# Sinkhorn-sorted attention and a token mixer on one core: batch 1's V turned on TensorE, half of the first q loaded in fp32, q of batches 1 and 2 turned in full tiles, a new order

## The chip, the cores and the metric

The kernel runs on one core of a Trainium2 chip. Its time is device microseconds of one execution, the median of several runs. The engines are TensorE (PE in the profile, its weight loads PEld), VectorE (DVE), ScalarE (ACT), GpSimd (POOL) and SyncE (SP), which here only issues DMAs. Batches are counted from 0 in all that follows; the change's own short title counts them from 1 where it says "batches 2 and 3".

## The reference

```python
B, H, S, D = 4, 8, 768, 64          # n_blocks = 8, block = 96, all inputs fp32
P = sort_net                        # (B, H, 8, 8)
for _ in range(5):                  # Sinkhorn
    P = exp(P - P.max(-1)); P /= P.sum(-1) + 1e-9; P /= P.sum(-2) + 1e-9
k_sorted = einsum('bhij,bhjcd->bhicd', P, k_blocks)      # blocks of 96 tokens
v_sorted = einsum('bhij,bhjcd->bhicd', P, v_blocks)
scores = q_blocks @ k_sorted_blocks.T / sqrt(D)          # within each block
attn = softmax(scores)
x = (attn @ v_sorted_blocks)  ->  (B, S, H * D)          # (4, 768, 512)
wq, wk = x @ w_q, x @ w_k                                # (4, 768, 64)
mixed = (wq @ wk.T / sqrt(64)) @ x                       # over all tokens of a batch
out = relu(mixed) @ w_out                                # (4, 768, 512)
```

## The kernel before

All of the core's work is written as units, one letter each, and one string, `ORDER` (lines 18 to 48), lists the units of all engines; the program issues them in that sequence. Each engine works through its own units strictly in this order, and a unit waits only for the data and for the PSUM banks that it needs. A unit is written as letter, batch, number, and then, for a unit on TensorE, the first PSUM bank that it writes (capitals: `K21:3` is the K unit of batch 2, head pair 1, into banks 3 and 4) or the engine (`k21:D:3` takes it out with VectorE; A is ScalarE, G GpSimd, S the SP queue).

The units, in the order of one batch's path:

- `l` issues a load. Each tensor of a batch (q, k or v, 1.57 MB in fp32) is one DMA on POOL's queue that casts to bf16 on its way (`u_l`, line 206). Three buffers stand for each of q, k and v, so batch 3 uses batch 0's. `lp` and `lo` load the mixer's weights.
- `a`, `c`, `p`, `B`, `u`, `n`: Sinkhorn for all 32 matrices at once, VectorE and ScalarE taking turns, then `n` spreads the result to M (line 232), the matrices with which K and V are sorted. `Z` are filler matmuls without use for the result.
- `Q`, `q`: q of a pair of heads turned on TensorE, twelve transposes of half tiles (128x64) a pair, then taken out to QT. For batch 3, GpSimd copies each pair to a contiguous place (`C`, line 360), and an SP transposing DMA turns it (`D` with number 4 and up, line 364).
- `K`, `k`: k sorted and turned in one go, twelve matmuls a pair against M, and taken out to KT.
- V goes one of two ways. In batch 0, `Y` does for V what `K` does for k (into the other batch's KT buffer), and `F` turns it back with eight transposes, `f` takes it to VT. In batches 1 to 3, `V` sorts it without turning (three units of eight matmuls), `v` takes it to Vs, and six SP DMAs `R` (line 301) rearrange it from Vs to VT; number n of `R` is one of six rows of 16 partitions, and every P of the batch needs all six.
- `S`, `e`: scores of five head-block pairs and their Exp on ScalarE. `P`, `r`, `x`: attention times V with a column of ones, its reciprocal and the product on VectorE.
- `T`, `t`: x turned on TensorE for batches 0 to 2; for batch 3 four SP transposing DMAs (`D` with numbers 0 to 3).
- `J`, `j`, `d`, `W`, `w`, `G`, `g`, `H`, `h`, `O`, `o`: the mixer; `O` and `o` give the output in six row groups of a batch, `s` stores them (`u_s`, line 434). `PAIRED` names the stores that go as one DMA of two row groups.

Queues to keep in mind: POOL issues all loads and in the same sequence makes M for later batches, the copies C and small copies d. SP issues all R, D and s, in order. In the old order the last lines of the loads are `lq2 .. lv3 .. lq3 .. lk3`: k of batch 3 is loaded last. On SP, the order near the last batch is `D37 R35 D36 R33 D35 R34 R32 D34`.

Of the kernel before, what the change touches and what calls it, by code (L numbers as in the profile page):

```python
# [22 lines left out]
n21:G e02:A:0 S01:6 f02:D:2 S06:3 e01:A:6 S00:0 n20:G F00:5 e06:A:3 V12:6 f00:D:5 e00:A:0 S04:2 lk2 v12:D:6
P01:4 e04:A:2 S05:0 lo r01:D:4 e05:A:0 R15:S P00:6 x01:D:4 lv2 S03:2 R14:S V10:0 e03:A:2 r00:D:6 lq2 P03:4
x00:D:6 v10:A:0 P04:2 lv3 r03:D:4 r04:D:2 K12:6 x03:D:4 P02:0 k12:A:6 x04:D:2 V11:4 r02:D:0 T03:7 x02:D:0
v11:A:4 T00:6 K11:2 t00:D:6 T01:0 R12:S lq3 k11:A:2 t03:D:7 T02:4 R11:S t01:A:0 Q13:6 Q11:7 lk3 R10:S Q12:5
t02:A:4 q11:D:7 Q10:0 R13:S K13:1 q10:A:0 J00:7 n31:G q12:A:5 S12:3 j00:D:7 J01:0 e12:A:3 k13:D:1 d00:G W00:7
j01:A:0 q13:D:6 K10:3 w00:A:7 d01:D n30:G k10:A:3 S14:0 S13:6 W01:2 e13:A:6 w01:D:2 K21:3 G00:2 e14:A:0
k21:D:3 S10:6 e10:A:6 K22:0 K20:3 k22:D:0 G01:2 k20:A:3 S11:6 g00:D:2 K23:0 e11:A:6 H01:2 k23:D:0 h01:A:2
P12:4 S16:6 S15:0 r12:D:4 e16:A:6 x12:D:4 P10:2 e15:A:0 O03:7 r10:D:2 x10:D:2 o03:A:7 V22:0 H00:4 v22:A:0  # L30
V20:6 h00:D:4 P11:2 v20:A:6 R25:S V21:0 r11:D:2 H02:4 x11:D:2 v21:A:0 R20:S P13:6 R21:S h02:A:4 r13:D:6 P14:0
x13:D:6 T11:2 R23:S Q20:3 R24:S Q21:4 r14:D:0 q20:A:3 Q23:7 R22:S q21:D:4 Q22:6 x14:D:0 S21:3 q22:A:6 O05:5
q23:D:7 e21:A:3 t11:D:2 T13:7 S22:0 t13:D:7 S20:3 e22:A:0 T12:6 O04:7 t12:D:6 e20:A:3 T10:6 o04:A:7 S24:0
t10:D:6 S26:2 O00:4 e26:A:2 o05:D:5 e24:A:0 V30:6 o00:A:4 S23:2 v30:D:6 S25:0 J10:5 e25:A:0 J11:4 R31:S
j10:A:5 P21:0 e23:A:2 R30:S d10:G W10:7 V32:5 r21:D:0 j11:A:4 x21:D:0 P23:2 w10:A:7 O02:4 v32:A:5 C31:G
r23:D:2 x23:D:2 P22:0 d11:A C33:G o02:A:4 P20:6 W11:5 r22:D:0 V31:2 x22:D:0 C30:G w11:A:5 D37:S O01:4 v31:A:2
C32:G r20:D:6 P24:0 x20:D:6 T22:5 o01:A:4 T21:2 R35:S t22:A:5 G10:3 r24:D:0 t21:D:2 D36:S K30:6 x24:D:0 K32:4
k30:A:6 G11:3 k32:D:4 K33:0 R33:S g10:A:3 K31:6 k33:A:0 D35:S H10:2 k31:D:6 T20:4 h10:A:2 T23:5 S35:0 R34:S
t23:D:5 S34:6 e35:A:0 H12:2 t20:D:4 R32:S O10:5 D34:S h12:A:2 J20:0 o10:D:5 e34:A:6 J21:1 j20:D:0 s00:S S36:4
s02:S S32:2 j21:D:1 S33:6 e36:A:4 s01:S W20:0 e32:A:2 d21:G P33:4 w20:D:0 d20:G O11:0 e33:A:6 r33:D:4 x33:D:4  # L40
W21:1 P34:2 w21:A:1 P32:6 r34:D:2 o11:A:0 x34:D:2 S31:4 G20:1 s10:S e31:A:4 r32:D:6 D33:S x32:D:6 S30:2 G21:1
H11:4 g20:A:1 D32:S P31:6 e30:A:2 O14:0 r31:D:6 x31:D:6 h11:A:4 P30:1 O15:3 o14:A:0 r30:D:1 D31:S x30:D:1
# [9 lines left out]
def kernel(  # L52
# [93 lines left out]
    def copy(e, o, i):  # L146
        if e == "A":
            nc.scalar.copy(o, i)  # L148
        else:
            nc.vector.tensor_copy(o, i)  # L150
# [34 lines left out]
    def u_i(b, n, e, bank):  # L185
# [9 lines left out]
        elif n == 3:  # L195
# [7 lines left out]
                nc.gpsimd.memset(t[:, :, :, D:DV], 1.0)  # L203
            nc.gpsimd.memset(Rall[:, :, NG - 1, :, (NU - AG * (NG - 1)) // 2:AG // 2], 1.0)

    def u_l(b, n, e, bank):
        if n == "p":
            for s, w in enumerate((moe_w_q, moe_w_k)):
                nc.gpsimd.dma_start(out=wqk[:, :, s, :], in_=w.rearrange("(t p) d -> p t d", p=P))  # L209
        elif n == "o":  # L210
            nc.gpsimd.dma_start(out=wo, in_=moe_w_out.rearrange("(t p) d -> p t d", p=P))  # L211
        else:
            t, src = {"q": (Qn, q), "k": (Kn, k), "v": (Vn, v)}[n[0]]
            h0, h1 = {"": (0, H), "a": (0, H // 2), "b": (H // 2, H)}[n[2:]]
            b = int(n[1])
            nc.gpsimd.dma_start(out=t[b % NIN][:, h0:h1].rearrange("p h r d -> p h (r d)"),  # L216
                                in_=src[b, h0:h1].rearrange("h (p r) d -> p h (r d)", p=P))
# [139 lines left out]
    def pairs(b, n):  # L357
        return Qn[(b + 1) % NIN].rearrange("p h r d -> p (h r d)")[:, n * 2 * R6 * D:(n + 1) * 2 * R6 * D]

    def u_C(b, n, e, bank):  # L360
        nc.gpsimd.tensor_copy(pairs(b, n).rearrange("p (r h d) -> p r h d", r=R6, h=2),
                              Qn[b % NIN][:, 2 * n:2 * n + 2].rearrange("p h r d -> p r h d"))

    def u_D(b, n, e, bank):
# [292 lines left out]
```

## Time and profile before

| | |
|---|---|
| time, median of 3 runs | 98.78 us (98.74 to 98.85) |
| the profiled execution | 99.26 us, of which the span is 97.4 us |
| granted TensorE clock, mean | 0.995 |
| busy: TensorE, VectorE, ScalarE, GpSimd | 84.3, 66.7, 70.7, 30.9 us |
| transfers: casting loads on POOL's queue | 14064 packets, 10.09 MB, 68.7% of 16 engines' span |
| transfers: SP's queue | 12064 packets, 10.31 MB, 39.2% |

The views of the profile that follow are: the page (busy time of each engine, the span in 40 slices, the chain that ended last); the chain in order of time (start, length, what); windows (busy time of each engine in a stretch, with instruction counts in brackets); groups of instructions (line, engine, operation, result and sources with shapes, count, then busy us and mean ns of one, then idle time before them and what ended it); the timeline (start us, length us, engine and line, count, in square brackets the idle time before it and what ended it); and the view of a tile (its instructions with their least, median and longest duration in ns, first and last start, and for DMAs the time from issue to landing). Buffer numbers are left out there: Qn, Kn and Vn are all buffers of q, k and v. All copies out of PSUM have the helper's lines, 148 for ScalarE and 150 for VectorE, and all matmuls line 144.

### The profile page before, as it was taken

The numbers are of one execution on the slowest core, as the hardware profiler recorded it, in microseconds if no ns is written. First come the engines' busy times: TensorE is split into PE (matmuls) and PEld (weight loads), VectorE is DVE, ScalarE is ACT, GpSimd is POOL, SyncE is SP. The second block draws the span as 40 slices with busy tenths as digits, with TensorE's granted clock in tenths as the row PEclk, the third lists the DMA queues.
The fourth block names the chain that finished last, engine by engine and source line by source line (L and its number), as shares of the span: only waits on it lengthen the run. The fifth ranks groups of instructions, "written<-read, shape, count | busy, mean of one in ns | idle before, by whom it ended". The sixth has DMA issues, their size and how long they took to land.

```text
span 97.4 us, 3326 instructions
## 1 busy us (share of the span) xinstructions
PE 84.3 (87%) x1396; PEld 58.2 (60%) x1406; DVE 66.7 (68%) x133; ACT 70.7 (73%) x102; POOL 30.9 (32%) x50
## 2 busy tenths in 40 slices
PE   4953978979898988988999999999899999999950
PEld 1323567868787576747965688984676545643410
DVE  2677985859993567879877569996596897625300
ACT  5411199999877899979789999899968644558450
POOL 5994009999406750000000086000300480000000
PEclk9999999999999999999999999999999999999997
DMA  0799999999999999999999999788999893691983
GB/s 3 76 197 203 203 205 208 199 204 204 207 221 205 235 248 205 204 204 206 211 249 250 222 201 235 131 170 101 295 423 312 90 247 142 252 391 73 398 315 120
DMA packets 26144, 20.62 MB, mean 212 GB/s; under 512 B 8336, under 2 KB 23440, under 8 KB 26128
## 3 DMA queue, kind: packets, MB, share of 16 engines
q0 software_dynamic: 14064, 10.09, 68.7%
q1 hardware_dynamic: 12064, 10.31, 39.2%
q8 instruction: 11, 0.18, 0.7%
q14 instruction: 5, 0.04, 0.1%
HBM read 20.19 MB, written 6.29 MB: 272 GB/s over the span
## 4 chain that ended last, share of the span: by engine, by line
PE 44%; DMA 32%; POOL 9%; ACT 5%; issue 3%; SPq 2%; DVE 1%; ACTq 0%; POOLq 0%; DVEq 0%
PE ps L144 44%; DMA Vn<-in_v_dram 20%; DMA Qn<-in_q_dram 8%; POOL M L240 5%; DMA VT<-Vs 4%; ACT KT L148 2%; POOL wqk L209 2%; SPq L366 1%; DVE mixT L421 1%; ACT ot L148 1%; ACT Vs L148 1%; ACT QT L148 1%; POOL Kn L216 1%; SPq L302 1%; POOL wo L211 1%
## 5 line engine op out<-in xcount | busy, mean ns | idle before, releaser
L316 ACT ACTIVATE E<-ps 96x960 bf16<-96x960 f32 (+1 forms) x28 | 24.1, 897 | 1.7 <-PE ps L144 1.4
L144 PE MATMUL ps<-wo,mixT 128*128 128x512 bf16 x87 | 22.3, 379 | 0.8 <-issue 0.3
L345 DVE TENSOR_TENSOR X<-ps,Rall 96x896 bf16<-96x896 f32 (+1 forms) x20 | 20.0, 1005 | 0.6
L144 PEld LDWEIGHTS <-mixT 128*128 128x128 bf16 x96 | 8.3, 97 | 9.2 <-issue 0.8
L148 ACT COPY ot<-ps 128x512 f32<-128x512 f32 x17 | 9.9, 586 | 4.8 <-PE ps L144 4.3
L144 PE MATMUL ps<-VT,E 96*128 96x65 bf16 x256 | 10.9, 193 | 1.0 <-DMA VT<-Vs 0.4
L144 PEld LDWEIGHTS <-E 96*128 96x128 bf16 x256 | 9.5, 97 | 3.1 <-issue 2.1
L382 POOL COPY qD<-qkT 64x384 bf16<-64x384 bf16 x4 | 2.0, 502 | 29.0 <-ACT qkT L148 20.1
L148 ACT CAST KT<-ps 128x768 bf16<-128x768 f32 x12 | 9.3, 804 | 1.4 <-PE ps L144 1.0
L240 POOL TENSOR_TENSOR M<-PTR,m_p 128x512 bf16<-128x512 bf16 x6 | 7.8, 1310 | 7.3 <-ACT KT L148 6.1
L144 PEld LDWEIGHTS <-KT 64*128 64x128 bf16 (+1 forms) x288 | 8.3, 97 | 2.9 <-issue 1.2
L144 PE MATMUL ps<-QT,KT 64*128 64x96 bf16 x256 | 9.2, 204 | 0.0
L150 DVE CAST KT<-ps 128x768 bf16<-128x768 f32 x8 | 7.6, 955 | 2.1 <-PE ps L144 2.0
L144 PE MATMUL ps<-M,Kn 128*64 128x128 bf16 x192 | 7.5, 220 | 1.4 <-DMA Kn<-in_k_dram 0.4
L419 ACT ACTIVATE mixT<-ps 128x1024 bf16<-128x1024 f32 x8 | 8.2, 1025 | 0.6 <-PE ps L144 0.6
L150 DVE COPY ot<-ps 128x512 f32<-128x512 f32 x7 | 4.8, 690 | 4.0 <-PE ps L144 3.7
L148 ACT CAST Vs<-ps 128x1024 bf16<-128x1024 f32 x7 | 6.9, 1017 | 0.9 <-PE ps L144 0.8
L144 PEld LDWEIGHTS <-Kn 128*64 128x64 bf16 x192 | 6.3, 109 | 2.0 <-DMA Kn<-in_k_dram 0.8
L144 PE MATMUL ps<-fil 128*128 128x512 bf16 x21 | 6.3, 464 | 1.4 <-DVE fil L192 1.2
L144 PE MATMUL ps<-idb,Qn 128*64 128x128 bf16 x144 | 4.8, 220 | 2.8 <-DMA Qn<-in_q_dram 2.8
L421 DVE TENSOR_SCALAR mixT<-ps 128x1024 bf16<-128x1024 f32 x4 | 4.8, 1222 | 2.5 <-PE ps L144 2.3
L144 PEld LDWEIGHTS <-Qn 128*64 128x64 bf16 x144 | 4.1, 110 | 3.9 <-DMA Qn<-in_q_dram 3.4
(80 smaller groups left out, 130.8 us busy)
## 6 DMA issues: line engine op xcount, KB each, us to landing
out_dram<-ot SPq DMA_DIRECT2D x18, 256.0 KB, 2.2
Qn<-in_q_dram POOLq DMA_DIRECT2D x4, 768.0 KB, 22.5
Vn<-in_v_dram POOLq DMA_DIRECT2D x4, 768.0 KB, 18.0
Kn<-in_k_dram POOLq DMA_DIRECT2D x4, 768.0 KB, 16.9
VT<-Vs SPq DMA_DIRECT2D x18, 132.0 KB, 6.3
out_dram<-ot SPq DMA_DIRECT2D x3, 512.0 KB, 4.3
wo<-in_moe_w_out_dram POOLq DMA_DIRECT2D x1, 512.0 KB, 16.7
wqk<-in_moe_w_q_dram POOLq DMA_DIRECT2D x1, 64.0 KB, 14.3
```

The lines of the kernel that those rows point to most:

```text
L144: nc.tensor.matmul(o, w, x, is_transpose=t, start=start, stop=stop, skip_group_check=True)
L148: nc.scalar.copy(o, i)
L150: nc.vector.tensor_copy(o, i)
L209: nc.gpsimd.dma_start(out=wqk[:, :, s, :], in_=w.rearrange("(t p) d -> p t d", p=P))
L211: nc.gpsimd.dma_start(out=wo, in_=moe_w_out.rearrange("(t p) d -> p t d", p=P))
L216: nc.gpsimd.dma_start(out=t[b % NIN][:, h0:h1].rearrange("p h r d -> p h (r d)"), in_=src[b, h0:h1].rearrange("h (p r) d -> p h (r d)", p=P))
L240: ENG[e].tensor_tensor(out=M[b % 2][:, h0:h0 + hn], in0=src.unsqueeze(2).to_broadcast([P, hn, SP, NB]), in1=m_p.unsqueeze(1).unsqueeze(3). ...
L316: nc.scalar.activation(E[b % 2][:, n, 0:2 * w * BLK].rearrange("p (t a c) -> p a t c", a=2, c=BLK), PS[0:BLK, bank:bank + 2, 0:w * BLK].re ...
L345: nc.vector.tensor_mul(xo.rearrange("p (a t d) -> p a t d", a=2, d=D), avps(bank, w)[:, :, :, 0:D], Rall[:, b, n, :, 0:w].unsqueeze(3).to_ ...
L382: nc.gpsimd.tensor_copy(o, i)
L419: nc.scalar.activation(o, i, ACT.Relu)
L421: nc.vector.tensor_relu(o, i)
```

## The change

1. V of batch 1 goes the way of batch 0: `Y`, `y`, `F`, `f` in place of `V`, `v` and the six `R`.
2. q of batch 0 is loaded in halves. Heads 0 to 3 come as fp32 on ScalarE's DMA queue (`lf`) into a mixer buffer that is free then; ScalarE casts them, two heads a copy (`X00`, `X01`). Heads 4 to 7 come as before (`lq0b`, POOL's queue, cast on the way).
3. The pairs in `WIDE` (pairs 0 and 1 of batch 0, all of batches 1 and 2) lie with their two heads side by side and are turned by six full-tile transposes in place of twelve half tiles. For batches 1 and 2 GpSimd's copy `C` lays them side by side, into XT's buffer.
4. `ORDER` is new throughout. The loads now come as `lf lq0b lk0 lv0 lq1 lv1 lk1 lv2 lp lk2 lq2 lo lk3 lv3 lq3`, so q of batch 3 is last. POOL's sequence from the third load on is `i03 lv0 lq1 lv1 n11 n21 lk1 C11 C12 C10 n10 C13 lv2 n20 lp lk2 lq2 lo n30 lk3 n31 lv3 lq3`. SP's, near the last batch, is `R34 R30 R35 R33 D35 D37 D34 D36 R32 R31`, with the copies `C31 C30 C33 C32` ahead of the four D. Ahead of the first K stand nine fillers (`Z09`). Between VectorE and ScalarE the copies out of PSUM are dealt anew: output copies `o` 12 and 12 (before 7 on VectorE, 17 on ScalarE), `q` 8 on VectorE and 4 on ScalarE (6 and 6), `v` 3 and 3, `h` 5 and 7 (4 and 8), `f` 5 and 3, `y` 2 and 6, `t` 10 and 2 (9 and 3), `k` 6 and 10 (8 and 8).
5. Stores: batches 0 to 2 may go two row groups at a time; batch 2's and 3's go one by one. 18 store DMAs in place of 21.

```diff
-PAIRED = "02 01 10"
+WIDE = "00 01 10 11 12 13 20 21 22 23"

 ORDER = """
-i02:D lq0 Z03:0 c00:D i00:G Z03:0 a01:A lv0 c01:D p01:A lk0 Z03:0 a02:A lv1 c02:D Z04:0 lk1 a03:A c03:D i03:G
...
+i00:G i02:D lf lq0b Z04:0 c00:D lk0 a01:A p01:A c01:D B01:0 i03:G Z03:1 a02:A lv0 c02:D Z03:1 X01:A lq1 a03:A
+Z03:1 X00:A lv1 c03:D p00:A:0 Q01:0 a04:A c04:D Z06:1 a05:A Z03:1 c05:D Q00:1 Q02:2 Q03:7 q02:A:2 B00:3
+q03:A:7 Z09:4 n00:D:3 n03:D:3 q00:A:1 n01:D:3 n02:D:3 u00:D:3 q01:D:0 K03:6 n11:G K00:2 k03:D:6 K02:0 k00:A:2
+K01:4 k01:D:4 Y02:6 k02:A:0 Y03:2 y02:A:6 S05:0 n21:G y03:D:2 Y01:4 e05:A:0 S04:6 y01:D:4 Y00:2 lk1 e04:A:6
...
+x14:D:0 O05:4 v30:D:2 V31:0 R34:S P20:6 v31:A:0 O00:5 R30:S r20:D:6 x20:D:6 R35:S C31:G o05:A:4 T13:2 R33:S
+S25:0 S26:3 t13:D:2 C30:G P22:6 e25:A:0 D35:S J10:2 r22:D:6 C33:G o00:A:5 x22:D:6 P23:0 j10:A:2 C32:G J11:5
+e26:A:3 D37:S r23:D:0 W10:7 x23:D:0 T20:6 d10:G j11:A:5 P24:2 t20:A:6 T21:4 D34:S W11:5 r24:D:2 w10:D:7 T22:0
+d11:A x24:D:2 S32:6 w11:A:5 G10:1 D36:S t22:D:0 e32:A:6 K32:2 t21:D:4 G11:1 k32:D:2 R32:S T23:7 g10:A:1 S35:4
+R31:S t23:D:7 H11:0 S31:2 e35:A:4 h11:D:0 s00:S J21:7 s01:S e31:A:2 s02:S J20:6 j21:D:7 S30:0 j20:D:6 S33:2
+d21:G H10:4 e30:A:0 W20:7 O12:6 h10:D:4 e33:A:2 P31:0 w20:D:7 o12:A:6 S36:4 S34:2 r31:D:0 d20:D e36:A:4 O13:7
...
 """

+    def wide(b, n):
+        return f"{b}{n}" in WIDE.split()
+
+    def abreast(b, n):
+        return XT[b % 2][:, n, :]
+
+    def stage():
+        return mixT[0].rearrange("p a c r s -> p (a c r s)").bitcast(FP32)
+
+    def u_X(b, n, e, bank):
+        w = 2 * R6 * D
+        i = stage()[:, n * w:(n + 1) * w]
+        if wide(b, n):
+            nc.scalar.copy(abreast(b, n).rearrange("p (r h d) -> p r h d", r=R6, h=2),
+                           i.rearrange("p (h r d) -> p r h d", h=2, r=R6))
...
     def u_l(b, n, e, bank):
...
+        elif n == "f":
+            nc.scalar.dma_start(out=stage().rearrange("p (h x) -> p h x", h=H // 2),
+                                in_=q[0, 0:H // 2].rearrange("h (p r) d -> p h (r d)", p=P))

     def u_Q(b, n, bank):
+        if wide(b, n):
+            for r in range(R6):
+                mm(bf(bank)[:, r * P:(r + 1) * P], abreast(b, n)[:, r * P:(r + 1) * P], idb, t=True)
+            return

     def u_C(b, n, e, bank):
-        nc.gpsimd.tensor_copy(pairs(b, n).rearrange("p (r h d) -> p r h d", r=R6, h=2),
+        nc.gpsimd.tensor_copy((abreast if wide(b, n) else pairs)(b, n).rearrange("p (r h d) -> p r h d", r=R6, h=2),
                               Qn[b % NIN][:, 2 * n:2 * n + 2].rearrange("p h r d -> p r h d"))

     def u_o(b, n, e, bank):
-        copy(e, oslot(b, n)[:, n % 2, :], PS[:, bank, :])
+        o, w = oslot(b, n)[:, n % 2, :], DM // len(e)
+        for i, x in enumerate(e):
+            copy(x, o[:, i * w:(i + 1) * w], PS[:, bank, i * w:(i + 1) * w])

     def u_s(b, n, e, bank):
-        if f"{b}{n}" in PAIRED.split():
+        if b < B - 1 and n < 3:
             ENG[e].dma_start(out=od[:, 2 * n:2 * n + 2, :], in_=oslot(b, 2 * n))
-            return
-        for m in (n,) if b == B - 1 else (2 * n, 2 * n + 1):
+        else:
+            m = n if b == B - 1 else n - 3
             ENG[e].dma_start(out=od[:, m, :], in_=oslot(b, m)[:, m % 2, :])
```

More of the change, by code (lines that the diff above doesn't have):

```diff
@@ L23 @@
[L23 to L42, printed above, removed]
@@ new lines @@
+Z03:1 X00:A lv1 c03:D p00:A:0 Q01:0 a04:A c04:D Z06:1 a05:A Z03:1 c05:D Q00:1 Q02:2 Q03:7 q02:A:2 B00:3
+q03:A:7 Z09:4 n00:D:3 n03:D:3 q00:A:1 n01:D:3 n02:D:3 u00:D:3 q01:D:0 K03:6 n11:G K00:2 k03:D:6 K02:0 k00:A:2
+K01:4 k01:D:4 Y02:6 k02:A:0 Y03:2 y02:A:6 S05:0 n21:G y03:D:2 Y01:4 e05:A:0 S04:6 y01:D:4 Y00:2 lk1 e04:A:6
+F02:0 S01:4 f02:D:0 y00:A:2 S06:6 F01:1 C11:G e01:A:4 S00:2 F03:0 C12:G e00:A:2 f03:D:0 C10:G e06:A:6 S03:4
+f01:D:1 P03:2 e03:A:4 n10:G S02:6 r03:D:2 F00:0 x03:D:2 e02:A:6 P04:4 Q11:1 C13:G f00:A:0 r04:D:4 P02:6
@@ L204, in u_i @@
             nc.gpsimd.memset(Rall[:, :, NG - 1, :, (NU - AG * (NG - 1)) // 2:AG // 2], 1.0)
+    def wide(b, n):
[11 more added lines that the diff above has]
+        else:
+            nc.scalar.copy(Qn[0][:, 2 * n:2 * n + 2].rearrange("p h r d -> p (h r d)"), i)
     def u_l(b, n, e, bank):
@@ L615 @@
         b, n = int(name[1]), int(name[2:])
-        if kind.isupper() and kind not in "RDC":
+        if kind.isupper() and kind not in "RDCX":
             fns[kind](b, n, int(arg[0]))
```

27 lines of the change are left out of this document (19 added, 8 removed).

## The prediction, made before the changed kernel ran

> **What bounds the kernel now.** First the page: the span, the busy shares, the slices of transfer time, the chain by engine.
>
> ```profile
> span 97.4 us, 3326 instructions
> PE 84.3 (87%) x1396; PEld 58.2 (60%) x1406; DVE 66.7 (68%) x133; ACT 70.7 (73%) x102; POOL 30.9 (32%) x50
> ...
> DMA  0799999999999999999999999788999893691983
> GB/s 3 76 197 203 203 205 208 199 204 204 207 221 205 235 248 205 204 204 206 211 249 250 222 201 235 131 170 101 295 423 312 90 247 142 252 391 73 398 315 120
> ...
> PE 44%; DMA 32%; POOL 9%; ACT 5%; issue 3%; SPq 2%; DVE 1%; ACTq 0%; POOLq 0%; DVEq 0%
> ```
>
> No engine's share of the whole span says what ends a stage, but the slices (2.4 us each) show one stage: from the third to the 25th the transfer engines are full, moving about 203 GB/s where only the casting loads run. So I read next the chain in order of time (start, length, what).
>
> ```profile
> 1.27 7.52 DMA Qn<-in_q_dram
> ...
> 22.79 19.85 DMA Vn<-in_v_dram
> ...
> 42.69 2.40 PE ps L144 x42
> ...
> 65.80 3.73 DMA VT<-Vs
> 69.53 0.25 issue
> 69.78 0.81 PE ps L144 x15
> ```
>
> Until 42.6 us the chain hangs on input loads, then on TensorE's order, and once more on a transfer: the last rearranging DMA of batch 3's V (batches count from 0 here), landed at 69.53. The last batch's first P starts behind it at 69.78. The windows before and after that P:
>
> ```profile
> core 0: us, PE busy (x) PEld busy (x) DVE busy (x) ACT busy (x) POOL busy (x), PEclk, DMA share, GB/s
> 12.60:69.80 57.20, 52.22 (x1084) 41.15 (x1090) 43.47 (x72) 51.95 (x71) 20.24 (x23) 1.00 1.25 207
> 69.80:94.00 24.20, 23.55 (x228) 12.78 (x232) 14.81 (x23) 14.81 (x25) 3.41 (x8) 1.00 0.85 265
> ```
>
> In the middle ScalarE is busy 51.95 of 57.20 us (91%), VectorE 43.47 (76%); in the tail only TensorE is full (23.55 of 24.20). I counted TensorE's units from that first P to the end in both orders: 2 S, 5 P, 3 W, 4 G, 7 H, 2 J, 17 O. They are the same, and the granted clock is 1.00 in both windows. So the tail should again take 97.4 - 69.8 = 27.6 us, and the question is when that P may start.
>
> **The load chain.** The loads stand in one POOL queue, one behind another. The views of the three input tiles give first and last issue and the landing times (the longest belongs to the last load of each).
>
> ```profile
> L216 POOL DMA_DIRECT2D Vn<-in_v_dram x4: 881/901/909, 2.9 to 25.3; - x4
> DMA to landing us min/median/max: 9.7/18.0/26.5
> L216 POOL DMA_DIRECT2D Qn<-in_q_dram x4: 876/908/1133, 1.3 to 30.1; - x4
> DMA to landing us min/median/max: 7.5/22.5/26.8
> L216 POOL DMA_DIRECT2D Kn<-in_k_dram x4: 883/893/950, 3.9 to 30.9; - x4
> DMA to landing us min/median/max: 12.6/16.9/31.2
> L302 SPq DMA_DIRECT2D VT<-Vs x18: 546/597/1706, 23.1 to 65.8; - x18
> DMA to landing us min/median/max: 2.5/6.3/7.9
> ```
>
> The first three loads end at 8.8, 2.9 + 9.7 = 12.6 and 3.9 + 12.6 = 16.5 us: 3.85 us each, undisturbed. V of batch 2 ends at 22.79 + 19.85 = 42.6, q of batch 3 at 30.1 + 26.8 = 56.9, k of batch 3, the last, at 30.9 + 31.2 = 62.1. The last four take 19.5 us, 4.1 more than 4 x 3.85; in that time some nine VT DMAs (batch 2's six, three of batch 3) and a first transpose share the engines. My estimate from that is 0.43 us of load time for each VT DMA.
>
> The change moves this chain in three ways. Half of the first q leaves the queue: -1.9 (half of 3.85). The other half is issued behind the identity's two POOL instructions, which today stand between the first two issues: 2.9 - 1.3 - 1.13 = 0.5, so +0.5. Batch 1's six VT DMAs go: -2.6. The last load, now q of batch 3, lands at 62.1 - 1.9 + 0.5 - 2.6 = **58.1**.
>
> The -1.9 needs the fp32 half to run in time that is idle now. The best slice moves 423 GB/s, the second slice 76: that slice alone has room for 2.44 x 347 = 0.85 MB, and the half is 0.79 MB. But where it runs beside the other half nothing is gained, just as loads beside VT DMAs stretched from 3.85 to 4.9 us. So 0 to 1.9 are the bounds; I take 1.9, since the room is there. The Trainium skill states the adverse side as a rule (Trainium Kernel Development and Optimization, Key Constraints): DMAs from the SP, ScalarE and GpSimd queues all run on the same 16 engines, and issuing from several only saves issue time. By that rule q lands at 60.0; the trace agrees where transfers overlap, and says nothing for engines that are idle.
>
> **From q's landing to the P.** In the old order k is last and q's turning starts five microseconds earlier. Now q's landing is followed by POOL's copies C and SP's transposes D, and behind these on SP's queue stand the last two VT DMAs, R32 and R31, for which every P of batch 3 waits. POOL's and SP's timeline price it:
>
> ```profile
> 56.97 3.13 POOL L361 COPY Qn<-Qn  128x768 bf16<-128x768 bf16 x4 [0.24 <-DMA Qn<-in_q_dram]
> 58.59 1.32 SPq L366 DMA_TRANSPOSE QT<-Qn  x1
> ...
> 63.80 1.32 SPq L366 DMA_TRANSPOSE QT<-Qn  x1
> 65.17 1.22 SPq L302 DMA_DIRECT2D VT<-Vs  x2
> 66.44 1.86 SPq L366 DMA_TRANSPOSE QT<-Qn  x1
> ```
>
> A copy takes 0.8. D35 follows the first (+0.9 after q's landing), D37 the third (+2.5), then it is 1.3 a transpose and 1.9 at worst for the last: D36 is issued by +6.4 to +7.0, R32 takes 0.6, R31 starts at +7.0 to +7.6. It lands 2.5 to 3.7 us later (the least of the VT view; the chain's own value): 9.5 to 11.3 after q. From 58.1 that is 67.6 to 69.4, middle 68.5, against 69.53 now. **The gate moves forward by 1.0 us.** It breaks even with q landing at 59.1.
>
> **Can the engines be there by then?** Rows that price the other parts:
>
> ```profile
> L148 ACT CAST KT<-ps 128x768 bf16<-128x768 f32 x12 | 9.3, 804 | 1.4 <-PE ps L144 1.0
> L148 ACT CAST Vs<-ps 128x1024 bf16<-128x1024 f32 x7 | 6.9, 1017 | 0.9 <-PE ps L144 0.8
> L148 ACT COPY ot<-ps 128x512 f32<-128x512 f32 x17 | 9.9, 586 | 4.8 <-PE ps L144 4.3
> L150 DVE COPY ot<-ps 128x512 f32<-128x512 f32 x7 | 4.8, 690 | 4.0 <-PE ps L144 3.7
> L421 DVE TENSOR_SCALAR mixT<-ps 128x1024 bf16<-128x1024 f32 x4 | 4.8, 1222 | 2.5 <-PE ps L144 2.3
> L150 DVE COPY QT<-ps 128x768 bf16<-128x768 bf16 x6 | 3.3, 551 | 1.5 <-PE ps L144 1.5
> L150 DVE COPY VT<-ps 96x1024 bf16<-96x1024 bf16 x4 | 2.6, 682 | 1.9 <-PE ps L144 1.9
> 8.83 1.20 PE L144 MATMUL ps<-idb,Qn 128*64 128x128 bf16 x36 [2.50 <-DMA Qn<-in_q_dram]
> 15.00 1.12 PE L144 MATMUL ps<-idb,KT 128*96 128x128 bf16 x16
> 26.83 0.61 PE L144 MATMUL ps<-Vn,M 128*128 128x128 bf16 x8 [0.21 <-DVE X L345]
> 6.33 0.26 ACT L160 ACTIVATE Pm<-Pm 32x64 f32<-32x64 f32 x1 [1.51 <-DVE Pm L181]
> L240 POOL TENSOR_TENSOR M<-PTR,m_p 128x512 bf16<-128x512 bf16 x6 | 7.8, 1310 | 7.3 <-ACT KT L148 6.1 <-PE ps L144 1.2
> ```
>
> *V of batch 1.* 24 V matmuls go (three times 0.61, 1.8 us). In come 48 Y in half tiles (as Q's, 1.20 for 36, so 1.6) and 32 F (two times 1.12, 2.2): TensorE +2.0. ScalarE gives up two evacuations of 1.02 and takes four y of 0.80 and two f. A 96x1024 bf16 copy on ScalarE isn't in the trace; it lies between 0.80 (768 wide) and 1.02 (1024 wide, fp32), and I take 1.02 for the width: ScalarE +3.2. VectorE gives one v and takes two f of 0.68: +0.1.
>
> *Full tiles for q.* Six matmuls stand for twelve. The full kind is 0.61 for 8, so 0.46 a pair of heads; the half kind 1.20 for 36, so 0.40. I count nothing on TensorE (bounds -0.6 to +0.6 over ten pairs). Eight more POOL copies of 0.8 come, 6.3 us on an engine with 66 us free. But C11 to C13 wait on POOL for q of batch 1, and behind them stand the issues of v2, the weights, k2 and q2. By the load rhythm q1 lands near 19; with four copies (3.1) and one M product (1.3), v2 is issued near 24, and v1 and k1 keep the transfers busy to about 26. So nothing, with 2 us in hand; past that an idle microsecond of loading is a microsecond of the gate.
>
> *ScalarE's first stage.* The two fp32 copies X (0.8 each, as the 768-wide cast) stand between Sinkhorn's Exps, where ScalarE is idle 1.51 us at a time. The first hides if the half lands by 5.5 (6.33 - 0.8); later, Sinkhorn slips by the excess. The nine fillers ahead of the first K run while M is made and cost at most the 1 us or so by which they outlast it; the loads gate what follows, so I count 0.
>
> *Evacuations.* VectorE takes over five o of 0.69, two q and one t of 0.55, one h and two v of 1.22 (h's row, same size), and gives up one f of 0.68: +8.1. Cut at the two windows: the five o and minus one h belong to the tail, and two q more than these fall into the middle, since the old order had them ahead of 12.6. The middle gets +7.1 with the V part: 43.5 becomes 50.6. ScalarE loses five o of 0.59 and more; its middle comes to 48 to 50. TensorE's middle is 52.2 + 2.0, but its busy time overstates (a full tile is 0.61 / 8 = 0.08 in a row). The fullest was held 91% busy; 50.6 at 91% is 55.6 us, and the P could start at 68.2, just ahead of the transfers' 68.5. Three engines and the transfers are then balanced, with nothing in hand.
>
> **Sum.** Last load -4.0, what q needs behind it +3.0: gate -1.0; tail 0. The profiled execution took 99.26 us with a span of 97.4 (1.86 around it). It would be 98.3 with a span of 96.4, and the median of 98.78 becomes **97.8**. (About 0.2% is what a measurement can tell from no change.)
>
> **Rivals.** (1) *VectorE becomes the bound: slower.* For the forecast it must be 50.6 / 55.9 = 91% busy where it was 76%. ScalarE's 91% says that an engine can be held there; against it, all r, x and most other links between two P groups are VectorE's, in order. It decides below 50.6 / 57.2 = 88%: at 85% the middle takes 59.5, the P starts at 72.1, and the kernel takes 98.78 + 2.4 = 101.2. Chance 0.24. (2) *The two halves run together:* 1.9 is lost, q lands at 60.0, the gate at 70.4: 99.7. The empty slices speak against it; 0.07. (3) *It moves nothing that shows:* half of the 1.9 goes, q lands at 59.1: 98.8; 0.13. (4) *The loads gain more:* VT DMAs without loads beside them land in 2.5, and the first slices take the whole half sooner, so that the gate is near 66.7 and the time 96.0. For it: the long VT landings stand beside loads. Against it: the engines must then do the middle in 54. Chance 0.18. The forecast itself, 97.0 to 98.5, has 0.38.
>
> **Numbers.** Faster 0.38 + 0.18 = 0.56, same 0.13, slower 0.24 + 0.07 = 0.31. The range leaves out the far half of rival 1 and some of rival 4: 95.8 to 100.2.
>
> **What the profile after would show.** Right: twelve VT DMAs; batch 0's V landing near 15; q of batch 3 at 57 to 59; R31 behind four transposes, landing at 67.6 to 69.4; 27.6 us from the first P of batch 3 to the end; VectorE's middle near 50. Wrong: TensorE waiting for VectorE through the middle; the fp32 half landing after 5.5, or the next Exp waiting for X; POOL waiting for q1 with idle transfer engines; or a tail of another length.

## The result and the profile after

The changed kernel takes 102.88 us (median of four executions) against 98.81 for the kernel before on the same chip: 1.038 times as long, 95% interval 1.028 to 1.047, which is 3.7 us (2.8 to 4.6) more. Here and below a median is over all executions, and a ratio leaves out those that fell in a slower state of the chip, here the one of 103.96 us beside 102.23, 102.38 and 103.39. The forecast was 97.8. The profiled execution is the one of 103.39 us, with a span of 101.6, so its trace shows 4.1 to 4.2 us more than the one before, somewhat above the mean loss.

The page first, with the lines that answer to those of before:

```profile
span 101.6 us, 3352 instructions
PE 87.3 (86%) x1411; PEld 60.2 (59%) x1411; DVE 74.3 (73%) x145; ACT 67.3 (66%) x96; POOL 37.6 (37%) x59
...
DMA  2899999999999999999999924789980668776782
GB/s 33 298 181 184 190 203 205 204 204 205 133 163 189 200 206 203 199 217 249 247 203 203 175 63 112 156 150 89 365 340 6 149 143 329 308 264 256 303 321 111
...
DMA 39%; PE 37%; POOL 16%; ACT 2%; SPq 1%; issue 1%; DVE 0%; POOLq 0%; ACTq 0%
```

Two things are new. POOL has 16% of the chain, where it had 9%. And the transfer slices, 203 to 205 GB/s where casting loads run undisturbed, show 181 to 190 in the third to fifth (5.1 to 12.7 us), and 133, 163, 189 in the 11th to 13th (25.4 to 33 us), around the late issue of v of batch 2. The fp32 half itself had landed at 5.5 us, so the first of these low stretches lies behind it. b1_lf and f1_fill below, with the same half on the same queue, show 203 to 205 there; why the changed kernel does not stays open. The chain in order of time, in pieces:

```profile
5.28 16.06 DMA Qn<-in_q_dram
...
21.40 2.35 POOL XT L387 x3
...
25.80 0.89 POOL Vn L238
...
33.26 18.56 DMA Kn<-in_k_dram
...
51.86 10.51 PE ps L145 x198
...
65.83 4.67 DMA QT<-Qn
...
70.55 27.24 PE ps L145 x276
```

q of batch 1 lands, POOL copies it, POOL then issues v of batch 2; later the chain runs over a transposing DMA of batch 3's q, 4.67 us long. The windows on both sides of batch 3's first P, which starts at 74.08 (before 69.78):

```profile
13.40:74.00 60.60, 55.28 (x1118) 43.26 (x1115) 49.66 (x81) 48.82 (x66) 27.13 (x31) 1.00 1.14 190
74.00:98.20 24.20, 23.77 (x228) 12.60 (x225) 17.11 (x28) 12.31 (x20) 4.23 (x9) 1.00 0.67 236
```

The columns are, as before: the window, its length, then busy time of TensorE, its weight loads, VectorE, ScalarE, GpSimd, the clock and the transfers. From that P to the end it takes 101.59 - 74.08 = 27.5 us, before 27.6. The whole loss lies ahead of the P. The same views of the tiles and queues as in the prediction:

```profile
L238 POOL DMA_DIRECT2D Qn<-in_q_dram x4: 893/921/1007, 1.5 to 37.2; - x4
DMA to landing us min/median/max: 3.3/5.8/22.3
L328 SPq DMA_DIRECT2D VT<-Vs x12: 546/602/1693, 40.3 to 70.1; - x12
DMA to landing us min/median/max: 2.3/5.2/8.6
```

q of batch 3, the last load, lands at 37.2 + 22.3 = 59.5 (forecast 58.1). The timeline of POOL and SP behind it, then that of TensorE up to the P:

```profile
59.54 3.13 POOL L387 COPY Qn<-Qn 128x768 bf16<-128x768 bf16 x4 [13.96 <-DMA Qn<-in_q_dram]
59.13 3.90 SPq L328 DMA_DIRECT2D VT<-Vs  x4
63.13 5.31 SPq L392 DMA_TRANSPOSE QT<-Qn  x4
68.49 2.22 SPq L328 DMA_DIRECT2D VT<-Vs  x2
```

```profile
66.91 0.39 PE L145 MATMUL ps<-QT,KT 64*128 64x96 bf16 x10 [1.20 <-DMA QT<-Qn]
...
70.55 0.39 PE L145 MATMUL ps<-QT,KT 64*128 64x96 bf16 x10 [0.94 <-DMA QT<-Qn]
70.86 1.47 PE L145 MATMUL ps<-XT,wqk 128*128 128x384 bf16 x8
...
74.08 0.60 PE L145 MATMUL ps<-VT,E 96*128 96x65 bf16 x14
```

When q lands, SP is still issuing four R (R34, R30, R35, R33) until 63.0: they wait for V's evacuations, the last of which ends at 60.9, and the issue of R33 alone then takes 1.69 us, where most take 0.6. So the first transpose D35 goes out 3.65 us behind q, not 0.9. D34 is issued at 65.83 and landed at 70.50. R31 lands at 72.5, but TensorE, which stood before S31 until D34's q was there, still had 3.5 us of units ahead of the P.

### The profile page after: what moved, and what is told of

Same layout as the page of the kernel before. It is cut to its first block, busy times and chain, and to the rows that moved or that the text cites. A ratio compares the mean times of both kernels' runs of the same rounds, so it can differ in the third digit from the quotient of the medians.

```text
span 101.6 us, 3352 instructions
## 1 busy us (share of the span) xinstructions
PE 87.3 (86%) x1411; PEld 60.2 (59%) x1411; DVE 74.3 (73%) x145; ACT 67.3 (66%) x96; POOL 37.6 (37%) x59
## 4 chain that ended last, share of the span: by engine, by line
DMA 39%; PE 37%; POOL 16%; ACT 2%; SPq 1%; issue 1%; DVE 0%; POOLq 0%; ACTq 0%
PE ps L145 37%; DMA Kn<-in_k_dram 18%; DMA Qn<-in_q_dram 16%; DMA QT<-Qn 5%; POOL M L262 4%; POOL XT L387 3%; POOL Qn L238 2%; POOL Kn L238 2%; POOL Vn L238 2%; POOL wqk L228 1%; SPq L392 1%; ACT ot L149 1%; POOL E L198 1%; POOL qD L408 1%; POOL wo L230 0%
## 5 line engine op out<-in xcount | busy, mean ns | idle before, releaser
L149 ACT CAST KT<-ps 128x768 bf16<-128x768 f32 x16 | 12.2, 805 | 2.8 <-PE ps L145 2.7
L145 PEld LDWEIGHTS <-KT 64*128 64x128 bf16 (+1 forms) x320 | 10.1, 100 | 5.7 <-DMA QT<-Qn 2.6
L408 POOL COPY qD<-qkT 64x384 bf16<-64x384 bf16 x5 | 2.5, 501 | 25.4 <-ACT qkT L149 17.1
L149 ACT COPY ot<-ps 128x512 f32<-128x512 f32 x12 | 7.0, 585 | 5.1 <-PE ps L145 5.1
L445 ACT ACTIVATE mixT<-ps 128x1024 bf16<-128x1024 f32 x7 | 6.9, 1020 | 4.6 <-PE ps L145 3.7
L145 PE MATMUL ps<-fil 128*128 128x512 bf16 x31 | 8.6, 427 | 1.2 <-DVE fil L193 1.2
L151 DVE COPY ot<-ps 128x512 f32<-128x512 f32 x12 | 8.2, 687 | 2.1 <-PE ps L145 1.9
L387 POOL COPY Qn<-Qn 128x768 bf16<-128x768 bf16 x4 | 3.1, 827 | 14.0 <-DMA Qn<-in_q_dram 14.0
L387 POOL COPY XT<-Qn 128x768 bf16<-128x768 bf16 x8 | 6.3, 818 | 2.8 <-DMA Qn<-in_q_dram 2.8
L145 PE MATMUL ps<-idb,XT 128*128 128x128 bf16 x60 | 4.7, 219 | 3.0 <-ACT m_p L149 3.0
L447 DVE TENSOR_SCALAR mixT<-ps 128x1024 bf16<-128x1024 f32 x5 | 6.1, 1224 | 1.5 <-PE ps L145 1.4
```

Source lines behind the costliest of these rows:

```text
L145: nc.tensor.matmul(o, w, x, is_transpose=t, start=start, stop=stop, skip_group_check=True)
L387: nc.gpsimd.tensor_copy((abreast if wide(b, n) else pairs)(b, n).rearrange("p (r h d) -> p r h d", r=R6, h=2), Qn[b % NIN][:, 2 * n:2 * n ...
L408: nc.gpsimd.tensor_copy(o, i)
L445: nc.scalar.activation(o, i, ACT.Relu)
L447: nc.vector.tensor_relu(o, i)
```

## The experiments

Theory F: the last load and the copies, transposes and R behind it set that P. Theory V: VectorE does (the first rival of the forecast). Later came E (the engines' orders hold it back whatever lands when), T (TensorE's own work) and S (the added work of the three computing engines together); L, C and D are explained where they come. All times are medians; ratios are to the kernel before in the same set of runs. Differences to the changed kernel are taken from the ratios; they are uncertain by about 1 us, since the changed kernel's own ratio is 1.028 to 1.047.

### Waits that the new order makes

**v of batch 2 loaded early** (a1_feed), in the changed kernel:

```diff
-... Y00:2 lk1 e04:A:6 ... q11:D:1 lv2 Y11:2
+... Y00:2 lk1 lv2 e04:A:6 ... q11:D:1 Y11:2
```

> The changed kernel with one load issue moved: lv2 (V of batch 2) goes on POOL's queue right behind lk1, ahead of the copies C11 to C13 that wait there for q of batch 1. Theory F (the last load and what follows it set the gate): the load engines had a hole from about 26 to 30 us because lv2 was issued at 25.75 while k of batch 1 was done by 29.0; with it filled, V of batch 2 lands near 32.5 in place of 33.7, q of batch 3 near 58.0 in place of 59.5, and the time falls by 1.0 to 1.5 us, to 101.4 to 101.9. Theory V (VectorE bounds the middle): loads that come earlier change nothing, 102.5 to 103.2.

Measured: 100.99 us, ratio 1.018 (1.012 to 1.023). That is 2.0 us off, more than theory F asked for, though within the uncertainty. The POOL timelines of the changed kernel and of this one show what was moved:

```profile
21.40 2.35 POOL L387 COPY XT<-Qn 128x768 bf16<-128x768 bf16 x3 [1.08 <-DMA Qn<-in_q_dram]
23.73 1.30 POOL L262 TENSOR_TENSOR M<-PTR,m_p 128x512 bf16<-128x512 bf16 x1
24.99 0.81 POOL L387 COPY XT<-Qn 128x768 bf16<-128x768 bf16 x1
25.75 0.94 POOL L238 DMA_DIRECT2D Vn<-in_v_dram  x1
```

```profile
18.33 0.94 POOL L238 DMA_DIRECT2D Kn<-in_k_dram  x1
19.26 0.89 POOL L238 DMA_DIRECT2D Vn<-in_v_dram  x1
21.06 2.36 POOL L387 COPY XT<-Qn 128x768 bf16<-128x768 bf16 x3 [0.90 <-DMA Qn<-in_q_dram]
```

The load was issued 6.5 us earlier and q of batch 3 landed at 58.4 instead of 59.5. V's "no change" falls here already: VectorE's work is the same. The trace's P came at 71.5 instead of 74.1, but that is not the edit's alone: in this execution sort_net, the small load that Sinkhorn starts from, landed at 2.4 us, in the changed kernel's at 3.5.

**Two R behind the transposes** (a2_sp), in the changed kernel:

```diff
-R34:S R30:S R35:S R33:S D35:S D37:S D34:S D36:S R32:S R31:S
+R34:S R30:S D35:S D37:S D34:S D36:S R35:S R33:S R32:S R31:S
```

> The changed kernel with two DMAs moved on SP's queue: R35 and R33 now stand behind the four transposes D35, D37, D34, D36 in place of ahead of them. Theory F: D35 starts right behind the first copy C31 (60.4 us) and not at 63.1, D34 lands near 68 and not at 70.5, S31 starts there; the last R lands near 72, so the first P of batch 3 starts near 72 in place of 73.9: 1.5 to 2 us less, 101.0 to 101.5. Theory V: VectorE's work is the same, no change, 102.5 to 103.2. If the slow issue of one R (1.7 us in place of 0.6) comes again elsewhere in the queue, the gain is about 1 us.

Measured: 101.84 us, ratio 1.029 (1.026 to 1.033), so 0.8 off, which is not clear of the noise. D34 landed at 67.4 instead of 70.5, and the P came at 71.9, 12.0 behind q's landing instead of 14.6. R31 landed at 71.8, and TensorE finished the unit ahead of the P at 71.9 as well, so this run does not tell which of the two set the P.

**Both edits** (c1_both):

> The changed kernel with both earlier edits at once: the load of v of batch 2 right behind that of k of batch 1, and the two rearranging DMAs R35 and R33 behind the four transposes of batch 3's q. Theory F (the last load, q of batch 3, and the chain C, D, R behind it set the first P of batch 3): the two gains add, 1.9 + 1.0, so the last load lands at 58.4 to 58.9, the first P of batch 3 starts at 69.5 to 70.3, and the time is 99.2 to 100.0. Theory E (the engines, which go through their orders one unit behind another, would not be there before about 71 even with q turned early): the first P starts at 71 or later and the time is 100.5 to 101, no better than with the load moved alone.

Measured: 100.61 us, ratio 1.019 (1.014 to 1.025). The last load landed at 58.3, R31 at 70.3, the P came at 70.41. F had the landing right and the time 0.6 too low; E had the time. Whether the P waited for R31 isn't shown: TensorE worked on the unit ahead of it, O12, until 70.39, and the chain of this run names TensorE there. Beside a1_feed alone (ratio 1.018) the second edit gives nothing that shows: the two gains do not add.

**No full tiles for batches 1 and 2** (c3_half): the units C10 to C13 and C20 to C23 are gone.

```diff
-WIDE = "00 01 10 11 12 13 20 21 22 23"
+WIDE = "00 01"
```

> The changed kernel without the full tiles for q of the second and third batch (numbers 1 and 2): their eight copies C on POOL are gone, and q is turned in half tiles, twelve matmuls for six. Theory F: what the full tiles cost is that POOL waits with its copies for q of batch 1 before it issues the load of v of batch 2; that issue comes at 21 to 22 instead of 25.8, no slices of idle transfer engines follow, the last load lands at 58.3 to 58.8 and the time is 100.5 to 101.3, as with the load moved alone. A rival (the full tiles spare TensorE time that counts): the gain in the loads is eaten by ten pairs of longer transposes, and the time is 101.8 to 102.8.

Measured: 101.39 us, ratio 1.022 (1.017 to 1.027). v of batch 2 was issued at 22.1, q of batch 3 landed at 58.2. That is 1.6 off the changed kernel, much as in a1_feed. So the full tiles gave nothing that shows, and their copies cost time through POOL's wait.

**Evacuations back on ScalarE** (c4_evac): o03, o02, h00, t10, q20, t12 and v20 from D to A.

> The changed kernel with seven evacuations of the middle (o03, o02, h00, t10, q20, t12, v20), 5.5 us in all, taken by ScalarE instead of VectorE. Theory V (rival 1 of the forecast: VectorE has become the bound): the first P of batch 3 comes earlier by 1 to 3 us and the time is 99.5 to 101.5. Theory F: the loads and the chain behind q stay where they were, the first P stays near 74 and the time is 102.0 to 103.0.

Measured: 104.43 us, ratio 1.053 (1.049 to 1.056), 1.5 slower than the changed kernel. V's forecast is refuted. F's zero is as well; that ScalarE has no room for 5.5 us either is the likely reason, which i2_act below bears out in the old order.

**The last two loads exchanged** (c2_q3), on top of a1_feed: `lk3 lq3 lv3`, with `C31 C33 C30 C32` and `D35 D37 D34` ahead of the first R.

> The changed kernel with v of batch 2 loaded early and, beside that, the last two loads exchanged (q of batch 3 ahead of v), its copies C and transposes D put ahead of the rearranging DMAs of batch 3's V on SP. This undoes the new order's choice that q is the last to land. Theory F: q lands near 54.6, the four transposes are issued by 61, V's last rearranging DMA R31 by 66 and landed by 69; the first P of batch 3 starts at 68.5 to 69.8 and the time is 98.0 to 99.3. Theory E: the first P is held near 71 by the engines whatever lands when, and the time is 100.2 to 101.

Measured: 103.85 us, ratio 1.054 (1.047 to 1.061), about 3 slower than a1_feed. q landed at 54.9 and R31 at 69.0, both as F said, but the P came at 73.1. In the trace TensorE waits 2.0 us for v, which was now last and stands before V32, and does not make it good. Early transfers alone do not bring the P forward.

### The fp32 half of the first q

**Without it** (a3_nolf), in the changed kernel: `lq0` in place of `lf lq0b`, no X, pairs 0 and 1 of batch 0 in half tiles.

> The changed kernel with the first q loaded whole on POOL's queue as in the kernel before (lf, lq0b and the two X copies gone; q of batch 0 turned in half tiles). As forecast (the fp32 half uses idle engines and takes 1.9 us of load time away): without it q of batch 3 lands 1.4 us later, near 60.9, and the time rises to about 104.3. Theory L (the fp32 half only displaces: sort_net landed 1.3 us later beside it and the first casting packet came at 4.6 in place of 3.1): sort_net lands near 2.3 again, Sinkhorn ends 1.2 us sooner, q of batch 3 lands within 0.7 of 59.5, and the time is 102.2 to 103.3.

Measured: 104.49 us, ratio 1.052 (1.046 to 1.058). The last load landed at 59.3, as with the half, so the half gives the loads nothing in the new order; yet without it the kernel was 1.5 slower than with it. Three windows of its trace show a reason (the number ahead of the last two is the granted clock):

```profile
68.20:70.20 2.00, 0.27 (x10) 0.24 (x10) 1.25 (x2) 0.77 (x1) 0.00 (x0) 1.00 0.70 100
70.20:73.60 3.40, 3.40 (x36) 1.83 (x32) 1.12 (x2) 1.17 (x2) 0.50 (x1) 0.54 1.00 375
73.60:76.00 2.40, 2.35 (x43) 1.49 (x40) 1.77 (x3) 2.29 (x4) 0.00 (x0) 0.95 0.50 203
```

TensorE stood idle for 1.75 us before D34's q, and then ran 3.4 us at about half its clock, right ahead of the P. From S31 to the P it took 5.15 us, in the changed kernel 3.53. These 1.6 us, less the 0.6 by which S31 came earlier, are the 1.0 us by which the P came later (75.08), and all that the two profiled executions differ by.

**It alone, in the kernel before** (b1_lf): `lf lq0b` for `lq0`, with X01 and X00 behind c02 and c03.

> The kernel before with only the fp32 half added: heads 0 to 3 of the first q on ScalarE's queue, cast by two ScalarE copies between Sinkhorn's Exps, heads 4 to 7 on POOL's queue first in the sequence; all else as before. As forecast: k of batch 3, the last load, lands 1.9 us sooner (60.2) and the time falls by 1 to 2 us, to 97 to 98. Theory L: sort_net lands at 3.6 in place of 2.3, the matrices M come 1.2 us later, the load chain gains at most 0.5 us, and the time is 98.5 to 99.8.

Measured: 99.19 us, ratio 1.003 (1.001 to 1.005). k of batch 3 landed at 59.6 instead of 62.1, as the forecast wanted; the time rose by 0.3. The clock is low here too: two windows of this run, and behind them the same two of the run g1_sp below, which has five fillers in the gap.

```profile
11.00:12.30 1.30, 0.03 (x2) 0.04 (x2) 1.16 (x6) 1.27 (x3) 0.00 (x0) 1.00 1.31 204
12.30:16.40 4.10, 3.51 (x61) 3.33 (x61) 2.11 (x6) 2.11 (x4) 1.76 (x2) 0.58 1.32 204
```

```profile
11.00:12.30 1.30, 1.25 (x11) 0.53 (x10) 1.16 (x6) 1.26 (x3) 0.00 (x0) 1.00 1.32 205
12.30:16.40 4.10, 3.14 (x74) 2.81 (x71) 2.75 (x8) 2.86 (x5) 1.89 (x2) 1.00 1.31 205
```

q is turned earlier, TensorE then waits for Sinkhorn with nothing to do, and the work behind runs at 0.58. The mean clock was 0.974 to 0.983 in all ten executions of this run, in the kernel before 0.994 to 1.000.

**With fillers in that gap** (f1_fill): `B01:0 Z05:1` in place of `B01:0`.

> The kernel before with the fp32 half of the first q alone (as in the run b1_lf), and five filler matmuls between the identity product and the sort product of TensorE's start. In that run TensorE was idle 1.28 us there, and its granted clock was 0.50 from 13 to 16 us. Theory C (the idle time is what lowers the clock, and that took back the gain of the loads): the clock stays at 1.00, batch 0's turning runs 1.2 to 1.6 us earlier, the first P of batch 3 starts at 67.7 to 68.4 and the time is 97.9 to 98.7, under the kernel before. A rival (TensorE and the transfers behind the last load decide, not the clock in the first stage): the first P stays at 68.7 and the time at 99.0 to 99.4.

Measured: 99.10 us, ratio 1.003 (1.000 to 1.006). The clock stayed up (0.983 to 1.000 in twelve executions), but the time is the rival's: theory C had the clock right and its price wrong. In the profiled execution Sinkhorn ended at 13.2 (12.2 in b1_lf, 11.9 before), because its small load had landed late, at 3.5. The timeline of VectorE's first step on sort_net, in the changed kernel, then in g1_sp:

```profile
3.62 0.21 DVE L172 TENSOR_REDUCE tmp<-Pm 32x8 f32<-32x64 f32 x1 [2.30 <-DMA Pm<-in_sort_net_dram]
```

```profile
2.39 0.21 DVE L171 TENSOR_REDUCE tmp<-Pm 32x8 f32<-32x64 f32 x1 [1.07 <-DMA Pm<-in_sort_net_dram]
```

**With the half on SP's queue, behind sort_net** (g1_sp), on top of f1_fill:

```diff
-            nc.scalar.dma_start(out=stage()...
+            nc.sync.dma_start(out=stage()...
```

> As the run f1_fill (before, with the fp32 half of the first q and five fillers), with the fp32 half issued on SP's queue right behind the small load of sort_net instead of on ScalarE's. In f1_fill sort_net landed at 3.5 us, 2.3 before, and Sinkhorn ended at 13.2 instead of 11.9. If the fp32 half's packets beside it are the cause: sort_net lands at 2.2 to 2.6, Sinkhorn ends at 11.8 to 12.2, the first P of batch 3 starts at 67.7 to 68.5 and the time is 97.9 to 98.5, under the kernel before. If the R behind the last load decide (R31 landed at 68.1 to 68.4 in both runs with the fp32 half): the P stays at 68.6 to 69.1 and the time at 98.7 to 99.2.

Measured: 98.33 us, ratio 0.9966 (0.9942 to 0.9990). sort_net landed at 2.3, Sinkhorn ended at 12.1 and the P came at 68.27, all as the expectation has it if the packets beside that load are the cause. This is the only version faster than the kernel before, by 0.3%.

**The same in the changed kernel** (h1_sp), on top of c1_both:

> As the run c1_both (the changed kernel with v of batch 2 loaded early and R35, R33 behind the transposes), with the fp32 half issued on SP's queue behind sort_net. There Sinkhorn ended at 12.8 and TensorE was idle only 2.2 us from then to the first P of batch 3, at 70.4. Theory T: Sinkhorn ends at 11.9 to 12.2 and everything behind it moves by that 0.6 to 0.9: the first P starts at 69.5 to 69.9, the time is 99.5 to 100.0. Theory F: the last load stays at 58.3 and R31 at 70.3, the P at 70.4, the time at 100.3 to 100.9.

Measured: 99.35 us, ratio 1.008 (1.005 to 1.011). The P came at 69.57, as T said. But the last load moved as well, to 57.2, and R31 landed at 69.5, so this run does not tell T from F. With three small edits about 2.9 of the 3.7 us are back.

### V of batch 1 on TensorE

**This part alone, in the kernel before** (b3_v1): Y10 to Y13, F10 to F13 and their evacuations for V10 to V12, v and six R. Two other kernels with this part, b2_v1 and d1_all, wrote an F into a bank whose P had not been read out; the kernel's guard on the row sums then took its slow path (75.5 ms), so they tell nothing of the change.

> The kernel before with one part alone: V of batch 1 turned on TensorE (four Y and four F for three V and six rearranging DMAs), everything else in the old order. Counted from the end of Sinkhorn to the first P of batch 3, TensorE was busy 52.8 of 57.9 us before, 55.6 of 60.9 in the changed kernel, and 55.4 of 57.7 with both edits of the run c1_both. Theory F (the transfers set that P): the six DMAs go, the last load lands 2 to 2.6 us earlier (59.5 to 60.1), the first P starts at 67.3 to 68.8 and the time is 96.6 to 98.0. Theory T (TensorE, whose matmuls follow one another with little idle time, sets it): 1.9 us more work and little idle time to put it in, the first P starts at 70.0 to 71.7 however early the loads land, and the time is 99.2 to 100.8.

Measured: 102.79 us, ratio 1.039 (1.037 to 1.041). The loads did even better than forecast, k of batch 3 landed at 58.0 instead of 62.1. It is 4.0 us slower all the same, about as much as the whole change loses; the P (71.4) is in theory T's range, the time above both. POOL's timeline shows that the early q was of no use:

```profile
58.28 0.50 POOL L382 COPY qD<-qkT 64x384 bf16<-64x384 bf16 x1 [19.71 <-ACT qkT L148]
58.84 3.13 POOL L361 COPY Qn<-Qn 128x768 bf16<-128x768 bf16 x4
```

q had landed at 52.0, but its copies stand on POOL behind d10 of batch 1's mixer, and POOL waited for that one's data until 58.28. The old order gives no way to use the gain: the stages ahead were later, and the copies with them.

**Both parts in the old order** (d2_all: g1_sp and b3_v1 together):

> The kernel before with both parts in the old order, k of batch 3 as the last load: the fp32 half on SP's queue with five fillers as in g1_sp, and V of batch 1 on TensorE as in b3_v1. Theory F: the gains of the loads add (last load at 57 to 58), the first P of batch 3 starts at 65.5 to 67.5, and the time is 95 to 97. Theory T: TensorE holds that P at 69.0 to 70.5, and the time is 98.3 to 99.8, more than g1_sp by 0.5 to 2.

Measured: 101.25 us, ratio 1.025 (1.023 to 1.027), 2.9 more than g1_sp. The last load landed at 57.2, as F said, the P came at 70.8, near T's end, and the time is above both.

**Only TensorE's share of the work** (i1_pe): before, with three times `Z03` ahead of P00, P02 and V11.

> The kernel before with nine filler matmuls more (1.95 us of TensorE at 0.22 each), three at each of three places between 24 and 32 us, and nothing else. Theory T (TensorE's own work between Sinkhorn and the first P of batch 3 sets that P): it moves by 1.2 to 2.0 us, and the time is 99.9 to 100.8. Rival S (ScalarE's and VectorE's evacuations, or the transfers, set it): the fillers go into idle time, the P stays within 0.4 and the time at 98.7 to 99.3.

Measured: 99.30 us, ratio 1.003 (1.000 to 1.005). T is refuted for work at these places: 1.95 us of matmuls cost 0.3.

**Work on ScalarE alone** (i2_act): before, with o00 to o04 copied twice.

> The kernel before with five of batch 0's output copies (o03, o04, o00, o02, o01) done twice by ScalarE, 2.9 us of its time between 40 and 62 us, and nothing else. Rival S (ScalarE, 91% busy in the middle before, carries the loss): the first P of batch 3 moves by 1.5 to 2.9 us and the time is 100.2 to 101.7. Theory T: it moves by 0 to 0.7, the time is 98.7 to 99.5.

Measured: 100.55 us, ratio 1.018 (1.015 to 1.022): 2.9 us of ScalarE cost 1.6 to 1.8. The time is in S's range; the P moved by 1.1 (70.86), less than S asked.

**The three engines' share without the dependencies** (i3_load): i1_pe, with k12, t02, t00, t03 and q11 also taken out twice.

> The kernel before with the work of V of batch 1 on TensorE, but without its dependencies: the nine fillers of i1_pe, two evacuations of ScalarE done twice (k12, t02: 1.6 us) and three of VectorE (t00, t03, q11: 1.65 us), all in the same stage, between batch 0's P and batch 1's S. V itself goes by the DMAs as before. Theory S (the sum of the work, on whichever engine is behind): the first S of batch 1, 14.7 us behind that of batch 0 before and 17.1 in b3_v1, comes 16.2 to 17.1 behind it, and the time is 100.3 to 102. Theory D (the chain Y, y, F, f that comes back to TensorE behind an evacuation): 14.7 to 15.5 behind it, and the time is 98.8 to 99.8.

Measured: 100.14 us, ratio 1.014 (1.008 to 1.020). The windows from batch 0's first S to batch 1's, in the kernel before, in this one, and in b3_v1:

```profile
18.00:32.70 14.70, 12.84 (x291) 10.79 (x288) 10.91 (x18) 12.67 (x16) 9.71 (x11) 1.00 1.37 208
```

```profile
18.20:34.80 16.60, 14.54 (x302) 11.66 (x300) 12.96 (x21) 14.28 (x18) 10.08 (x11) 1.00 1.35 208
```

```profile
18.00:35.00 17.00, 15.12 (x345) 12.71 (x344) 12.70 (x21) 13.30 (x18) 9.61 (x11) 1.00 1.36 202
```

The stage grows from 14.7 to 16.6 by the work alone and to 17.0 with the dependencies. So theory S holds for the stage, and D looks small; but the stand-in isn't exact: in its window ScalarE has 1.6 us more than before, in b3_v1's 0.6, so D's share may be larger than the 0.4 us between the two. The time of i3_load is 1.4 above before (0.8 to 2.0), just under S's range, that of b3_v1 4.0. Of the rest, the trace of b3_v1 shows 2.0 us behind the P: the last transposed x lands at 83.7 (before 80.5), TensorE waits for it, and the end comes 4.5 instead of 3.7 us behind the last matmul. No run takes that apart.

## Why the prediction was wrong

**The tail: right.** 27.5 us against 27.6.

**The last load: 1.4 us late, 59.5 for 58.1.** Two terms failed. The half was priced at its full 1.9 less 0.5 for the identity, but v of batch 0, the third load, landed at 16.7, not near 15: 1.6 lost. Without the half it was 16.4 and the last load 59.3 (a3_nolf), so in the new order the half gave nothing. The Trainium skill's rule that issuing from several queues only saves issue time (Trainium Kernel Development and Optimization, Key Constraints) bears on this. In the new order the runs agree with it. Measured alone, in the old order, it did not hold: the last load came 2.5 us earlier (b1_lf). And "nothing, with 2 us in hand" for POOL's copies was wrong: v of batch 2 was issued at 25.75, 3.2 us before k of batch 1 landed (29.0), and yet the rate fell to 133 GB/s in the slice from 25.4 on; moving that issue brought the last load forward by 1.1 (a1_feed). The prediction had named the wait and its price, and its cover was too short. In the other direction, three VT DMAs of batch 3 that ran beside loads before now go out when the last one has all but landed (from 59.13 on), which is 1.3 less at the estimate of 0.43 each. 58.1 + 1.6 + 1.1 - 1.3 is the measured 59.5.

The price of 0.43 for a VT DMA itself held: k of batch 3, with six of them beside it, took 6.3 us instead of 3.85, 0.41 each. In b3_v1 seven of them went out ahead of the last load's landing, in the kernel before fifteen; the load came 4.1 earlier for that, 0.5 for each of the eight.

**From q's landing to the P: 14.6 us for 10.4, the larger failure.** The sum let D35 go out 0.9 behind q. SP was at four other R until 63.0, whose places stand in the new order, and the sum left them out; so R31 landed 13.0 behind q, not 10.4. The sum then ended with R31's landing, while the P also stood behind S31, its q and 3.5 us of TensorE's units, which ended 1.6 later still. With two of the four R moved (a2_sp, c1_both, h1_sp) the P came 12.0 to 12.4 behind q; what that is worth in time is not clear of the noise.

**Can the engines be there by then? The test was the wrong one.** VectorE's 50.6 was near (49.66), ScalarE's 48 to 50 as well (48.82), and nothing on TensorE for full tiles too (c3_half). But the test asked whether one engine could be held at 91% of a 57 us window. What decides is each stage: between batch 0's and batch 1's first S, ScalarE was 86% busy and TensorE 87%, and nearly all the work put there made the stage longer (i3_load), though TensorE's part alone hardly showed (i1_pe). The same stretch of the changed kernel:

```profile
18.00:36.50 18.50, 16.86 (x380) 14.87 (x378) 15.07 (x25) 16.47 (x21) 16.46 (x18) 1.00 1.30 186
```

It is 3.8 us longer than before, with about 4 us more work on each of the three engines, and the P is 4.3 us later. That is not the price of V of batch 1 alone, since the new order also moves other units in (V20, V21, K10, two F and two Y of batch 0) and two out (J00, Q12). But the stretch behind it, up to the P, is not shorter for that: 37.6 us for 37.1, with 2.1 us in which TensorE waits for transposes of q and 1.1 for k of batch 3. In h1_sp it is 35.0. So the units behind came later, V's evacuations and the mixer's among them, and with these the R on SP (until 63.0 in the changed kernel) and the copies on POOL (from 58.8 in b3_v1). That is the likely reason why the part that freed the loads most, V of batch 1, lost most by itself.

**The rivals.** VectorE as the bound gave the right sign, and its 101.2 was the nearest number, for a reason that the runs do not bear out: it was 82% busy, the same work ran at 87% in h1_sp, and relieving it at ScalarE's cost made things worse (c4_evac). The two halves that run together fit the 1.6 us lost at the start, but not the rate behind the half's landing. That the loads gain more was right in b3_v1 and worth nothing there.

**What stays open.** The edits of h1_sp bring back about 2.9 us of the 3.7; they overlap, so they are no sum. V of batch 1 costs 4.0 alone in the old order, 2.9 beside the fp32 half, and what it costs in the new order was not measured by itself. Of its 4.0, about 1.4 (0.8 to 2.0) is shown to be work on three engines; that an order made for it, with the copies ahead of d10, would win the rest back wasn't tried.

## What to carry to other kernels

Do not stop a sum at the transfer that lands last: follow its successors through every queue they stand in, with what is queued ahead, and then the units that the waiting engine still has to do. Where several engines are 85% busy in a stage, price added work by the stage and by all engines at once, since taking transfers away there can lose more than it gains. A load that is issued behind a data wait on its queue needs its cover counted in microseconds (3.2 were not enough here), and a part that looks good belongs in the old order alone first.

## What the runs showed of the hardware

**The clock fell after short idle stretches.** TensorE idle for 1.28 us (b1_lf) and 1.75 us (a3_nolf) was followed by about 3.4 us at half clock. The gap's length alone does not tell: 2.50 us at 6.3 in the kernel before and 3.05 us at 5.7 in the changed one were followed by none, yet the same gaps, 2.00 us in i1_pe and 2.69 us in c4_evac, were followed by half clock in those traces. The Trainium skill (TensorE: Matmul & The Clock Gate, HAM oscillation) warns of gaps over some 3.4 us; here shorter ones did it, and five fillers, 1.1 us of work, prevented it (f1_fill, g1_sp).

**A small load can suffer beside a large one.** sort_net landed at 2.2 to 2.5 us in the nine traces without the fp32 half or with it behind on the same queue, and at 2.4 to 3.6 in the nine with the half on ScalarE's queue beside it: there it is delayed in some executions, by up to 1.3 us, and in others hardly at all. Sinkhorn starts that much later.
